# Retention attention and a capacity-limited expert layer on one core: the planned VectorE times behind each routing list, and the last eviction in two halves

## The chip, the cores and the metric

The kernel runs on one core of a Trainium2 chip, as one program. The metric is the device time of one execution in microseconds (us). Before the change three executions took 613.02, 613.28 and 613.60 us (median 613.28). The trace comes from one further execution under the hardware profiler: its own time was 615.13 us, its span (first to last recorded instruction) 613.3 us.

## The reference, cut to what matters

```python
scores = scale * np.matmul(q, k.transpose(0, 1, 3, 2))      # 8 batches, 8 heads, 576 positions, 64 wide
ret = scores * Dmat[None, :, :, :]                          # gamma_h ** (i - j) for i >= j, else 0
attn = np.matmul(ret, v)                                    # -> x, 4608 tokens x 512
logits = x @ w_gate                                         # 4608 x 8
for idx in np.argsort(-logits.flatten()):                   # best (token, expert) pair first
    tok, e = idx // E, idx % E
    if assigned[tok] >= 0 or counts[e] >= 576:              # a token once, an expert 576 times
        continue
    assigned[tok] = e; counts[e] += 1
for e in range(8):
    out[mask_e] = np.maximum(x[mask_e] @ w1[e], 0) @ w2[e]  # 512 -> 1024 -> 512
```

The order in which pairs are accepted is sequential in the reference. The kernel finds the same assignment by closing one expert at a time: eight searches, each followed by the list of the 576 tokens of the expert that it closed.

## The kernel before, in words

**Stages.** TensorE (PE) computes the attention in the first 130 us or so. Then it runs the experts e = 0 to 7, each as `l1(e)` and `l2(e)`. `l1` makes 16 groups of 12 matmuls (each float32 operand is split in a high and a low part, so that a product is three matmuls), 128x256 and 128x320 in turn, with relu on ScalarE (ACT, L1093) and the low part of the result on VectorE (DVE, `low`, L1056). `l2` makes five tiles `py` of 128x512 (the last of 64 rows); ACT copies each to `yt` (L1155; L1157 and DVE L1158 for the 64 rows), and GpSimd (POOL) scatters the rows to the output by an indirect DMA (L1113). The last expert takes its tiles in the order 4, 0, 1, 2, 3.

**Routing.** `phases()` is one long generator that alternates between DVE work and small bf16 matmuls on PE. For p = 0 to 6 a search runs: rounds `it` in which DVE builds a matrix of comparisons `G` (L174), PE sums it with 9 matmuls (L350, result `r`), and DVE decides (L354 to L366). Then the list of the expert found: DVE builds `rh` and `G`, PE runs L458 and L461 into `r`, DVE turns `r` into the row numbers `idx` (L468 to L472) and, for list 5 onwards, `quart` (L477, L479), by which POOL gathers the tokens. Then `leave(p)` (L504 to L515) takes the expert and its tokens out of play, and `best` (L208 to L220) finds each token's best expert that is left, which opens the next search.

**What sets the order.** Each `yield ns, pe` of the generator names a planned DVE time since the last yield, and a planned PE time of the matmuls behind it. A planner (`Mixer`) keeps two planned clocks, one for PE and one for DVE. After each few matmuls of `l1` and `l2` it advances the PE clock (`mix.adv`), and when the planned DVE clock says that the operands are ready it puts the generator's next small matmuls into PE's queue, and the DVE work behind them into DVE's queue. So the planned times alone decide after how many expert matmuls a routing matmul stands on PE, and what stands ahead of what on DVE. All queues run in the order written; nothing is reordered on the chip.

**The tokens of an expert.** Experts 0 to 4 have their tokens transposed on PE (`pt`, L1038; low part by DVE L1041). Experts 5 to 7 (`QUART` = 5) have them gathered in 18 quarter gathers and transposed on DVE in five pieces (four of 128x4x128, the last 128x4x64): DVE L1020 makes `xt`, ACT L1022 copies it to `xh`, and DVE L1013 subtracts to make `xl`, one piece behind. The pieces are put into the queues one by one during `l2` of the expert before when their planned arrival is past, and what is left is put there at the start of `l1` without a further condition. The first group of `l1` (256 tokens) needs pieces 0 and 1, the second (320 tokens) the others too.

Of the kernel before, what the change touches and what calls it, by code (L numbers as in the profile page):

```python
# [16 lines left out]
AF = mybir.ActivationFunctionType  # L17
# [4 lines left out]
N, DM, E, FF = 4608, 512, 8, 1024  # L22
SLACK = 1.0
QUART = 5
# [46 lines left out]
def widths(shifts):  # L71
    return [1 << (a - b) for a, b in zip([32] + shifts[:-1], shifts)]
# [16 lines left out]
class Route:  # L89
# [232 lines left out]
    def search(s, p):  # L322
        nc, V, pool, ps = s.nc, s.nc.vector, s.pool, s.ps
        SH, KK = LATER, widths(LATER)
        for _ in s.ordered():
            pass
        s.dig(0)
        for it, K in enumerate(KK):
            last = it == len(SH) - 1
            v2 = pool.tile([128, 36, 2], BF16, name="v", bufs=2)  # L330
            v = v2[:, :, 0]
            if it:

                V.tensor_scalar(v2, u[:, :, None].to_broadcast([128, 36, 2]), j, float(K), op0=ALU.subtract, op1=ALU.mult)
            else:
                V.tensor_copy(v2, s.dg[:, 0, :, None].to_broadcast([128, 36, 2]))
            s.reach(0, 36, K, v2, ALU.is_le)
            if it == 0:
                for k in range(1, 7):
                    s.dig(k)  # L340
                for a, b in ((1, 4), (4, 7)):
                    V.tensor_scalar(s.D[:, a:b], s.dg[:, a:b], 1.0/KK[a], None, op0=ALU.mult)
            if not last:
                u = pool.tile([128, 36], F32, name="u")
                V.tensor_tensor(u, v, s.D[:, it+1], op=ALU.add)

            yield (2050 + 19*K if it else 1350 if p > 1 else 350), 310
            cp = ps.tile([128, 32], F32, name="r")
            for c in range(0, 36, 4):
                nc.tensor.matmul(cp, s.G[:, c:c+4].rearrange("p c k -> p (c k)"), s.oh[:, c:c+4, :], start=(c == 0), stop=(c == 32))  # L350
            own = [cp[32*c:32*c+32, 8*c:8*c+8] for c in range(4)]

            cs = pool.tile([32, 8], F32, name="cs")
            V.scalar_tensor_tensor(cs, s.nr[:32], -1.0, own[0], op0=ALU.mult, op1=ALU.subtract)  # L354
            for x in own[1:3]:
                V.tensor_tensor(cs, cs, x, op=ALU.subtract)
            for q in range(0, 128, 32):
                V.tensor_tensor(s.f[q:q+32, :8], own[3], cs, op=ALU.is_ge)
            if last:
                break  # L360

            mq = pool.tile([128, 1], F32, name="mq")
            tc, j = pool.tile([128, 32], F32, name="tc"), pool.tile([128, 1], F32, name="j")
            V.tensor_reduce(mq, s.f[:, :8], axis=AX.X, op=ALU.max)
            V.transpose(tc, mq.to_broadcast([128, 32]))
            V.tensor_reduce(j, tc[:, 1:K], axis=AX.X, op=ALU.add)  # L366

        tf, cf = pool.tile([128, 32], F32, name="tc"), pool.tile([128, 32], F32, name="cf")
        nk, nf = pool.tile([128, 1], F32, name="nk"), pool.tile([128, 1], F32, name="nf")
        w = pool.tile([128, 8], F32, name="w8")  # L370
        s.ge = pool.tile([128, 2, 36], F32, name="ge")
        s.gt, s.eq = s.ge[:, 0], s.ge[:, 1]
        V.transpose(tf, s.f)
        V.tensor_reduce(nk, tf[:, :K], axis=AX.X, op=ALU.add)
        V.transpose(cf, nk.to_broadcast([128, 32]))
        V.tensor_reduce(nf, cf[:, :8], axis=AX.X, op=ALU.max)
        V.scalar_tensor_tensor(w, cf[:, :8], nf, s.dec, op0=ALU.is_equal, op1=ALU.mult)
        V.tensor_scalar(s.gt, v, nf, -1.0, op0=ALU.subtract, op1=ALU.is_gt)
        V.tensor_scalar(s.eq, v, nf, -1.0, op0=ALU.subtract, op1=ALU.is_equal)
        s.pick(w)  # L380
# [116 lines left out]
    def leave(s, p):  # L497

        nc, V, pool, ps = s.nc, s.nc.vector, s.pool, s.ps
        if p == 0:  # L500
            s.taken()
        e = pool.tile([128, 8], F32, name="eb")
        a = pool.tile([128, 36], F32, name="gone")
        V.tensor_scalar(e, s.es, -2*BIG, BIG, op0=ALU.mult, op1=ALU.add)  # L504
        V.scalar_tensor_tensor(a, s.q, CAP - HALF, s.mem[:, 1], op0=ALU.is_lt, op1=ALU.mult)
        V.tensor_tensor(s.Lg, s.Lg, e[:, None, :].to_broadcast([128, 36, 8]), op=ALU.min)
        V.tensor_tensor(a, a, s.gt, op=ALU.add)
        if p == 0:
            V.tensor_scalar(s.cap, a, -2*BIG, BIG, op0=ALU.mult, op1=ALU.add)
            V.tensor_tensor(s.acc, s.gt, s.mx8, op=ALU.mult)  # L510
        else:
            V.tensor_scalar(a, a, -2*BIG, BIG, op0=ALU.mult, op1=ALU.add)
            V.tensor_tensor(s.gt, s.gt, s.mx8, op=ALU.mult)
            V.tensor_tensor(s.cap, s.cap, a, op=ALU.min)
            V.tensor_tensor(s.acc, s.acc, s.gt, op=ALU.add)  # L515
        if p == 0:
            yield 1550, 100
            cn = ps.tile([128, 8], F32, name="r")
            nc.tensor.matmul(cn, s.ones, s.n8, start=True, stop=True)
        for _ in s.best(capped=True):  # L520
            pass
        if p == 0:
            s.room(cn)
        yield (2400 if p == 0 else 5000 if p == 1 else 3500 if p < QUART else 4700), 0

def attention(tc, nc, P, qk, vk, cst_d, er_d, wg_d, rf, xd, Lg):
    cst = P['a'].tile([128, CST], F32, name="cst")
# [376 lines left out]
def moe(tc, nc, P, R, xd, w1_d, w1q_d, w2_d, out, mix):  # L904
    V, A, T = nc.vector, nc.scalar, nc.tensor
# [66 lines left out]
    def conv(by=None):  # L972

        conv_hi()
        conv_lo(by)
# [143 lines left out]
    def l2(e, hb):  # L1119
        tr = iter(())  # L1120
        late = []
        want = 4*(e + 1 < E)
        wait = 0
        for t in range(5) if e < E - 1 else (4, 0, 1, 2, 3):
            n = 128 if t < 4 else 64
            ps = P['ps'].tile([128, DM], F32, name="py", tag="y", bufs=2)
            c = slice(128*t, 128*t+n)
            k, last = 0, 23 if t < 4 else 15
            for f in range(8):
                wh, wl = [w[:, (f % 2)*512:(f % 2)*512+512] for w in W2[e, f // 2]]  # L1130

                h = hb[:, f]
                for a, w in ((h[:, c], wh), (h[:, 640+128*t:768+128*t], wh), (h[:, c], wl)) if t < 4 else \
                        ((h[:, 512:640], wh), (h[:, c], wl)):
                    m = a.shape[1]
                    T.matmul(ps[:m], a, w, start=(k == 0), stop=(k == last), skip_group_check=True)  # L1136
                    k += 1
                mix.adv(650 if t < 4 else 430)
                if owed and f == 1:
                    owed.pop()()  # L1140
                gather(e + 1)
                wait -= 1

                soon = state['listing'] == e + 1 and not ready(e + 1)
                if want and wait <= 0 and e + 1 in regs and not soon:
                    conv()
                    want, wait = want - 1, 6
                if late and not soon:
                    late.pop(0)()
                if e + 1 in XG and e + 1 not in XH and mix.t > state['arrives']:  # L1150
                    tr = transposes(e + 1)
                next(tr, None)
            y = P['w'].tile([128, DM], F32, name="yt", bufs=3)
            if t < 4:
                A.activation(y, ps, AF.Copy)  # L1155
            else:
                A.activation(y[:n], ps[n:], AF.Copy)  # L1157
                V.tensor_tensor(y[:n], y[:n], ps[:n], op=ALU.add)  # L1158
            late.append(lambda t=t, y=y, n=n: scatter(e, t, y, n))
        if QUART - 1 <= e + 1 < E - 1:  # L1160
            behindhand.extend(late)
        else:
            for f in late:
                f()
        for _ in range(want):
            conv()
        if e + 1 < E:
            mix.drain(lambda: ready(e + 1))
            gather(e + 1, True)
            if e + 1 not in XH:  # L1170
                tr = transposes(e + 1)
        return tr
# [105 lines left out]
```

## Time and profile before

| | |
|---|---|
| three executions, median | 613.28 us |
| profiled execution, its own time | 615.13 us |
| its span | 613.3 us |
| PE busy | 597.1 us (97% of the span) |
| DVE busy | 421.0 us (69%) |
| ACT busy | 289.4 us (47%) |
| POOL busy | 187.9 us (31%) |

Experts' `l1` start on PE at about 222.6 (e = 1), 280, 338, 395.9, 451.74 (e = 5), 503.8 and 555 us. The lists' matmuls (L458) start at 202.6, 251.2, 298.5, 346.7, 395.25, 441.8 and 459 us for lists 1 to 7. In a matmul row of the timeline the duration includes the time to run through the array, so matmuls that follow each other start closer together than their rows are long (128x512 rows of 0.39 us follow each other by 0.23). Idle time in front of a row is counted from the modelled end of the one before. The execution's own time is 1.83 us longer than its span (615.13 − 613.3).

### The profile page before, as it was taken

The numbers are of one execution on the slowest core, as the hardware profiler recorded it, in microseconds if no ns is written. First come the engines' busy times: TensorE is split into PE (matmuls) and PEld (weight loads), VectorE is DVE, ScalarE is ACT, GpSimd is POOL, SyncE is SP. The second block draws the span as 40 slices with busy tenths as digits, with TensorE's granted clock in tenths as the row PEclk, the third lists the DMA queues.
The fourth block names the chain that finished last, engine by engine and source line by source line (L and its number), as shares of the span: only waits on it lengthen the run. The fifth ranks groups of instructions, "written<-read, shape, count | busy, mean of one in ns | idle before, by whom it ended". The sixth has DMA issues, their size and how long they took to land.

```text
span 613.3 us, 14831 instructions
## 1 busy us (share of the span) xinstructions
PE 597.1 (97%) x5711; PEld 509.9 (83%) x5715; DVE 421.0 (69%) x1545; ACT 289.4 (47%) x585; POOL 187.9 (31%) x260
## 2 busy tenths in 40 slices
PE   8999999998999999999999999999999999999995
PEld 5888887775698889879977998799889889989984
DVE  3688989898799878978886897799884323312300
ACT  4555555551364456433552447154536636634410
POOL 0000000000511442341432233257727746862121
PEclk9999999999999999999999999999999999999998
DMA  9999999924477699694988298649858995994611
GB/s 322 401 374 324 390 364 383 328 82 161 138 187 146 214 251 227 201 241 137 218 226 233 63 246 209 204 83 253 207 170 170 234 260 121 248 251 139 125 39 39
DMA packets 51504, 132.05 MB, mean 215 GB/s; under 512 B 6352, under 2 KB 20304, under 8 KB 51432
## 3 DMA queue, kind: packets, MB, share of 16 engines
q0 software_dynamic: 15296, 50.87, 37.5%
q1 hardware_dynamic: 35812, 79.77, 37.4%
q8 instruction: 45, 0.74, 0.5%
q10 hardware_dynamic: 324, 0.45, 0.2%
q14 instruction: 27, 0.22, 0.1%
HBM read 80.21 MB, written 18.87 MB: 162 GB/s over the span
## 4 chain that ended last, share of the span: by engine, by line
PE 74%; DVE 12%; issue 7%; DMA 3%; POOL 2%; ACT 1%; POOLq 0%; SPq 0%; ACTq 0%; DVEq 0%
PE ph L1083 24%; PE py L1136 24%; PE pA L598 6%; PE pX L642 5%; PE pS L621 3%; PE pX L633 2%; DVE hb L1056 2%; PE pT L680 2%; POOL xg L989 2%; PE r L350 1%; DMA out_y<-yt,idx 1%; DVE G L174 1%; PE pT L694 1%; PE pt L1038 1%; PE pXt L650 1%
## 5 line engine op out<-in xcount | busy, mean ns | idle before, releaser
L1136 PE MATMUL py<-w2h,hb 128*128 128x512 f32 x576 | 186.8, 396 | 0.0
L1083 PE MATMUL ph<-xh,w1h 128*128 128x320 f32 (+1 forms) x512 | 151.4, 301 | 0.7 <-issue 0.4
L1083 PE MATMUL ph<-xl,w1h 128*128 128x320 f32 (+1 forms) x512 | 148.6, 296 | 0.0
L1083 PE MATMUL ph<-xh,w1l 128*128 128x320 f32 (+1 forms) x512 | 148.5, 296 | 0.0
L1136 PE MATMUL py<-w2l,hb 128*128 128x512 f32 (+1 forms) x320 | 125.1, 391 | 0.0
L1136 PEld LDWEIGHTS py<-w2h,hb 128*128 128x128 f32 x576 | 104.9, 188 | 22.4
L1093 ACT ACTIVATE hb<-ph 128x256 fp32r<-128x256 f32 (+1 forms) x128 | 52.2, 408 | 104.8 <-PE ph L1083 94.5
L1083 PEld LDWEIGHTS ph<-xh,w1h 128*128 128x128 f32 x512 | 95.9, 189 | 2.4 <-issue 1.5
L1083 PEld LDWEIGHTS ph<-xl,w1h 128*128 128x128 f32 x512 | 96.1, 190 | 0.6 <-DVE xl L1041 0.3
L1083 PEld LDWEIGHTS ph<-xh,w1l 128*128 128x128 f32 x512 | 96.0, 190 | 0.0
L1056 DVE SCALAR_TENSOR_TENSOR hb<-ph,hb 128x256 fp32r<-128x256 f32 (+1 forms) x192 | 58.2, 352 | 45.7 <-ACT hb L1093 38.0
L989 POOL DMA_INDIRECT xg<-xd,idx x25 | 25.8, 1031 | 188.4 <-ACT w1h L957 153.8
L1113 POOL DMA_INDIRECT out_y<-yt,idx x40 | 40.5, 1012 | 89.7 <-ACT yt L1155 59.2
L1136 PEld LDWEIGHTS py<-w2l,hb 128*128 128x128 f32 (+1 forms) x320 | 56.7, 177 | 12.7
L1155 ACT ACTIVATE yt<-py 128x512 f32<-128x512 f32 x32 | 19.1, 596 | 86.6 <-PE py L1136 55.8
L1000 POOL DMA_INDIRECT xg<-xd,quart x54 | 54.6, 1011 | 15.3 <-issue 12.3
L967 POOL DMA_DIRECT2D w2l<-raw x32 | 30.1, 954 | 73.2 <-ACT hb L1093 72.5
L582 ACT ACTIVATE vin<-vin,cst 128x128 f32<-128x128 f32 (+1 forms) x160 | 48.2, 380 | 6.5 <-DMA vin<-in_vk 4.3
L600 DVE TENSOR_TENSOR am<-pA,cst 128x1024 f32<-128x1024 f32 x32 | 38.8, 1213 | 11.4 <-PE pA L598 11.1
L967 POOL DMA_DIRECT2D w1l<-raw x29 | 27.5, 963 | 43.5 <-ACT w1l L966 30.6
L598 PEld LDWEIGHTS pA<-qin,kin 64*128 64x128 f32 x512 | 31.6, 189 | 9.4 <-issue 3.5
L623 ACT ACTIVATE S<-pS 128x128 f32<-128x128 f32 x64 | 17.8, 278 | 42.9 <-PE pS L621 42.6
(193 smaller groups left out, 907.5 us busy)
## 6 DMA issues: line engine op xcount, KB each, us to landing
raw<-in_w SPq DMA_DIRECT2D x52, 512.0 KB, 5.4
w2l<-raw POOLq DMA_DIRECT2D x32, 512.0 KB
w1l<-raw POOLq DMA_DIRECT2D x29, 512.0 KB
kin<-in_qk SPq DMA_DIRECT2D x14, 576.0 KB
qin<-in_qk SPq DMA_DIRECT2D x14, 576.0 KB, 7.5
vin<-in_vk SPq DMA_DIRECT2D x14, 576.0 KB
nin<-in_vk SPq DMA_DIRECT2D x14, 512.0 KB, 8.7
xd<-xr SPq DMA_DIRECT2D x36, 192.0 KB, 7.8
```

The lines of the kernel that those rows point to most:

```text
L582: nc.scalar.activation(x, x, AF.Copy, scale=vs[:, u % HP, 4*c+h:4*c+h+1])
L598: nc.tensor.matmul(pa[:, r, j], LD[u, 'k'][half(r), s], LD[u, 'q'][half(r), s], start=True, stop=True, skip_group_check=True)
L600: nc.vector.tensor_tensor(AM[u, hf], pa, m1[:, None, None, :].to_broadcast([128, 2, 4, 128]), op=ALU.mult)
L642: nc.tensor.matmul(PX[u, hf][half(h), b, 128*c:128*c+128], v[:, a:a+64], AM[u, hf][:, h ^ b, j], start=False, stop=False, skip_group_check ...
L967: nc.gpsimd.dma_start(lo, raw, accum_op=ALU.add)
L989: nc.gpsimd.indirect_dma_start(out=xg[:n, 4*j:4*j+4, :].rearrange("p a c -> p (a c)"), out_offset=None, in_=xd[:, :], in_offset=bass.Indir ...
L1000: nc.gpsimd.indirect_dma_start(out=XG[e][:, g, :], out_offset=None, in_=xq, in_offset=bass.IndirectOffsetOnAxis(ap=lines[e][:, g:g+1], axi ...
L1056: V.scalar_tensor_tensor(hb[:, f, to+a:to+b], ps[:, a:b], 0.0, hb[:, f, 256*s+a:256*s+b].bitcast(F32), op0=ALU.max, op1=ALU.subtract)
L1083: T.matmul(ps, w, x, start=(k == 0), stop=(k == 11))
L1093: A.activation(hb[:, f, c], ps, AF.Relu)
L1113: st = nc.gpsimd.indirect_dma_start(out=out[:, :], out_offset=bass.IndirectOffsetOnAxis(ap=found[e][:n, t:t+1], axis=0), in_=y[:n], in_off ...
L1136: T.matmul(ps[:m], a, w, start=(k == 0), stop=(k == last), skip_group_check=True)
```

## The change

Four planned times change, none in the first lists: the first matmul of a search from p = 2 on is planned for 1500 instead of 1350 ns, the second round of a search from p = 3 on for 350 ns more. `leave` from p = 2 on gets a yield of 1100 ns ahead of its operations and another ahead of `best`, and its last yield becomes 1300 instead of 3500 (p = 2 to 4) or 2000 instead of 4700 (p = 5, 6). A yield with a PE time of 0 has no matmul behind it; it lets the planner put expert work between the pieces. And the last tile of the last expert is copied out in two halves, columns 0 to 255 by ACT, 256 to 511 by DVE.

```diff
-            yield (2050 + 19*K if it else 1350 if p > 1 else 350), 310
+            yield (2050 + 19*K + 350*(it == 1 and p > 2) if it else 1500 if p > 1 else 350), 310
@@ leave
         if p == 0:
             s.taken()
+        if p > 1:
+            yield 1100, 0
         e = pool.tile([128, 8], F32, name="eb")
@@ leave
             nc.tensor.matmul(cn, s.ones, s.n8, start=True, stop=True)
+        elif p > 1:
+            yield 1100, 0
         for _ in s.best(capped=True):
             pass
         if p == 0:
             s.room(cn)
-        yield (2400 if p == 0 else 5000 if p == 1 else 3500 if p < QUART else 4700), 0
+        yield (2400 if p == 0 else 5000 if p == 1 else 1300 if p < QUART else 2000), 0
@@ l2
-            if t < 4:
+            if t == 3 and e == E - 1:
+                A.activation(y[:, :DM//2], ps[:, :DM//2], AF.Copy)
+                V.tensor_copy(y[:, DM//2:], ps[:, DM//2:])
+            elif t < 4:
                 A.activation(y, ps, AF.Copy)
```

Line numbers up to 501 stay, then they grow by 2, by 4 from 520 on, and by 7 behind the changed lines of `l2`.

The rows below are instructions in the order in which they stand in an engine's queue. In DVE's queue, the list of expert 6 before the change (`r` is the matmuls' result, `lo`, `tk`, `idx` and `quart` make the row numbers, `eb` opens `leave`, `oh` ends `best`, `xt` and `xl` are expert 5's transposed tokens):

```order
L479 TENSOR_SCALAR quart<-tk 32x4x5 x4
L504 TENSOR_SCALAR eb<-es 128x8
...
L220 TENSOR_TENSOR oh<-t_536,mx_537 128x288
L1020 STREAM_TRANSPOSE xt<-xg 128x4x128
L1013 TENSOR_TENSOR xl<-xt,xh 128x4x128
L1020 STREAM_TRANSPOSE xt<-xg 128x4x64
L1013 TENSOR_TENSOR xl<-xt,xh 128x4x128
L1013 TENSOR_TENSOR xl<-xt,xh 128x4x64
L398 TENSOR_SCALAR w_7154<-room 128x8
```

And the same place after the change:

```order
L1024 STREAM_TRANSPOSE xt<-xg 128x4x128
L1017 TENSOR_TENSOR xl<-xt,xh 128x4x128
L494 TENSOR_TENSOR room<-room,r 128x8
...
L479 TENSOR_SCALAR quart<-tk 32x4x5 x4
L1024 STREAM_TRANSPOSE xt<-xg 128x4x64
L1017 TENSOR_TENSOR xl<-xt,xh 128x4x128
L1165 TENSOR_TENSOR yt<-yt,py 64x512
L1017 TENSOR_TENSOR xl<-xt,xh 128x4x64
L506 TENSOR_SCALAR eb<-es 128x8
```

The last piece of expert 5 stood behind list 6, `leave` and `best`, and stands directly behind the list now, with `leave` behind it. In PE's queue, the end of the same list's matmuls before the change (`n` is the count of tokens taken, `py` a tile of `l2(4)`):

```order
L458 MATMUL r<-rh,G 128x160
L461 LDWEIGHTS ones
L461 MATMUL r<-n_7019,ones 128x8
L1136 MATMUL py<-w2h,hb 128x512 x2
L1136 MATMUL py<-w2l,hb 128x512
```

And after the change (`ph` is the first group of `l1(5)`, 12 matmuls of 128x256, of which the first and the last are shown, and then the first two of the second group):

```order
L1140 MATMUL py<-w2l,hb 64x512
L458 LDWEIGHTS G
...
L461 MATMUL r<-n_7069,ones 128x8
L1087 MATMUL ph<-xh,w1h 128x256
...
L1087 MATMUL ph<-xh,w1l 128x256
L1087 MATMUL ph<-xh,w1h 128x320
L1087 MATMUL ph<-xl,w1h 128x320
```

The list's matmuls have moved from the middle of `l2(4)` to its end: what stands behind them is no longer `l2` but the first group of the next expert. At the end of the program, DVE and ACT after the change, with what each waits for (the numbers behind names are those of semaphores):

```order
L1165 TENSOR_TENSOR yt<-yt,py 64x512 [waits DMASW0_49,Activation_49]
L1160 COPY yt<-py 128x256 [waits DMASW1_49,DMASW2_49,DMASW0_49,Activation_49]
```

```order
L1162 ACTIVATE yt<-py 128x512 [waits DMASW7_49,DVE_49,PE_49]
L1159 ACTIVATE yt<-py 128x256 [waits DMASW0_49,PE_49,Activation_49]
```

The DVE half waits for an ACT instruction, and the ACT half for PE: the two halves stand one behind the other, where one ACT instruction of 128x512 (L1155) stood before.

## Rows read from the trace of the kernel before

**Rows 1.** Windows by stage; columns window, length, busy us of each engine, clock, DMA
```profile
250.00:350.00 100.00, 98.62 (x693) 84.21 (x693) 82.16 (x358) 44.25 (x69) 32.60 (x44) 1.00 0.71 186
350.00:450.00 100.00, 99.28 (x693) 86.37 (x692) 86.39 (x375) 47.10 (x73) 47.56 (x66) 1.00 0.81 205
450.00:600.00 150.00, 150.00 (x907) 135.65 (x906) 46.28 (x132) 70.81 (x115) 74.33 (x108) 1.00 0.68 170
```

**Rows 2.** Waits of PE between 250 and 450 us; total us, times, longest
```profile
PE r L350 <- DVE G L174: 1.2, 3, 0.7
PE r L350 <- issue: 0.3, 1, 0.3
PE ph L1083 <- DVE hb L1056: 0.2, 1, 0.2
PE ph L1083 <- issue: 0.2, 1, 0.2
PE pt L1038 <- DVE v L334: 0.2, 1, 0.2
```

**Rows 3.** Timeline of PE behind list 2; start, length, instruction, [idle before]
```profile
251.87 0.17 PE L461 MATMUL r<-n,ones 128*128 128x8 bf16 x1
...
258.58 0.39 PE L1136 MATMUL py<-w2l,hb 128*128 128x512 f32 x1
259.68 0.39 PE L350 MATMUL r<-oh,G 128*128 128x32 bf16 x9 [0.72 <-DVE G L174]
```

**Rows 4.** Timeline of PE, list 6 and the start of expert 5
```profile
442.49 0.71 PE L1136 MATMUL py<-w2h,hb 128*128 128x512 f32 x2
...
451.74 0.28 PE L1083 MATMUL ph<-xh,w1h 128*128 128x256 f32 x1
...
453.16 0.31 PE L1083 MATMUL ph<-xh,w1h 128*128 128x320 f32 x1
453.31 0.31 PE L1083 MATMUL ph<-xl,w1h 128*128 128x320 f32 x1
```

**Rows 5.** Timeline of DVE from list 6 on
```profile
442.69 0.16 DVE L494 TENSOR_TENSOR room<-room,r 128x8 f32<-128x8 f32 x1 [0.36 <-PE r L461]
...
444.97 0.74 DVE L479 TENSOR_SCALAR quart<-tk 32x20 int32<-32x20 f32 x4
...
450.34 0.43 DVE L1020 STREAM_TRANSPOSE xt<-xg 128x256 f32<-128x256 f32 x1
450.70 0.99 DVE L1013 TENSOR_TENSOR xl<-xt,xh 128x512 fp32r<-128x512 f32 x2
...
453.66 0.68 DVE L1158 TENSOR_TENSOR yt<-yt,py 64x512 f32<-64x512 f32 x1
```

**Rows 6.** Timeline of ACT at the start of expert 5
```profile
450.81 0.42 ACT L1022 ACTIVATE xh<-xt 128x256 fp32r<-128x256 f32 x1 [0.30 <-DVE xt L1020]
...
451.99 0.59 ACT L1157 ACTIVATE yt<-py 64x512 f32<-64x512 f32 x1 [0.27 <-ACT yt L1155]
453.42 0.38 ACT L1093 ACTIVATE hb<-ph 128x256 fp32r<-128x256 f32 x1 [0.84 <-PE ph L1083]
```

**Rows 7.** Timeline of all engines at the end, and a DVE read of 128x256 earlier
```profile
465.02 0.42 DVE L1056 SCALAR_TENSOR_TENSOR hb<-ph,hb 128x256 fp32r<-128x256 f32 x1 [0.99 <-ACT hb L1093]
...
606.04 0.60 ACT L1155 ACTIVATE yt<-py 128x512 f32<-128x512 f32 x1 [4.89 <-PE py L1136]
606.92 0.97 POOL L1113 DMA_INDIRECT out_y<-yt,idx  x1 [4.43 <-ACT yt L1155]
```

**Rows 8.** Windows behind PE's last matmul, columns as in the first group
```profile
606.00:610.00 4.00, 0.00 (x0) 0.00 (x0) 0.00 (x0) 0.60 (x1) 0.97 (x1) 0.98 0.17 66
610.00:613.30 3.30, 0.00 (x0) 0.00 (x0) 0.00 (x0) 0.00 (x0) 0.00 (x0) 0.50 0.00 0
```

**Rows 9.** Timeline of PE at the start of the program
```profile
1.48 3.17 PE L1224 MATMUL warm<-full 128*128 128x512 bf16 x7 [1.48 <-DVE full L1211]
...
6.32 0.82 PE L1224 MATMUL warm<-full 128*128 128x512 bf16 x3
```

## The prediction, made before the changed kernel ran

> **What bounds the kernel now.** I read the table of busy shares first: PE 97%, DVE 69%, ACT 47%, so the end is set by PE's queue, and the question is only where PE stands still. The windows by stage answer it [rows 1]: from 450 us on PE is busy for all of 150.00 us, between 250 and 450 it lacks 1.38 + 0.72 = 2.10 us. Nothing behind 450 us can absorb a delay, and nothing there can be gained either: what PE wins or loses before 450 us, or at any place after it, goes to the end one for one. The third view, PE's waits in these 200 us, has seven waits with 2.1 us in sum [rows 2]; four of them are at L350, the first matmuls of a search, which come just behind a list. The timeline of the longest [rows 3] shows that a wait is worth more than its bracket: matmuls of `l2` follow each other at 0.23 us (30 of them lie between 251.9 and 258.8), but their rows are 0.39 long, so from 258.58 the next could start at 258.81 and starts at 259.68, 0.87 later where the bracket says 0.72. With 0.15 more for each of seven, the waits cost 2.1 + 1.05 = 3.15 us. That is all that a better order of the routing can win.
>
> **The cause of the waits.** Behind list 2 PE has 30 expert matmuls in its queue, 6.9 us, and DVE needs from 251.87 to 259.68, 7.8 us, for the list's rows, `leave`, `best` and the first `G` [rows 3]. The planner believed less, so it put the search's matmul too early.
>
> **Part 1, the planned times.** They add no instruction; they move the small matmuls, and DVE's work with them, along the expert work. Counted in the changed queue, behind list 2 now stand 39 expert matmuls instead of 30: 39 × 0.23 = 9.0 us against the 7.8 needed, so that wait is gone. Behind list 3 the cover grows from 8.2 to 9.5 us, behind list 4 from 8.9 to 9.2, behind list 5 from 9.7 to 10.4 (numbers of matmuls times 0.12, 0.15 or 0.23 by their width). The DVE chain there also has `low` operations of 0.42 [rows 7] between its parts, and with lists 4 and 5 the new cover is only 0.3 and 0.7 longer. I leave 0.1 to 0.2 of wait at each of these two, and about 0.35 (0.2 by its bracket and 0.15) at a transposition on PE that waits behind the search on DVE [rows 2], which the new times don't touch: 0.65 in all. Gain 3.15 − 0.65 = **2.5 us**; the bounds are 3.15 (all waits gone) and 0 (each comes back elsewhere).
>
> **What the moves trigger.** The planned totals are longer now for each list, so everything behind list 2 drifts along the expert work. List 6's matmuls stood in the middle of `l2(4)`, 9.3 us ahead of expert 5 (442.49 to 451.74) [rows 4], and DVE had done the list, `leave`, `best` and the last two pieces of expert 5's tokens while PE worked on `l2(4)`. Now the list's matmuls are the last thing before `l1(5)`, and on DVE the last piece (128x4x64) stands behind the list's rows. The second group of `l1(5)` needs that piece. So PE must wait for DVE to do the whole list, and the price can be worked out from durations of before. Let S be the start of the matmul that stands directly behind L461: 442.49 in the trace, the first of `l1(5)` in the changed queue.
> DVE's first operation on the list starts 0.20 behind S (442.69), the last (`quart`) ends at 444.97 + 0.74 = 445.71, S + 3.22 [rows 5]. The piece's transposition takes 0.43: S + 3.65. ACT's copy to `xh` starts 0.04 later (450.34 + 0.43 to 450.81) and takes 0.42: S + 4.11 [rows 5, 6]. PE's 13th matmul, the first of the second group, is due at S + 1.42 (453.16 − 451.74) [rows 4]: it waits **2.7 us**.
> The 14th needs `xl` of that piece. DVE has the earlier piece's subtraction first (0.99 for the two of 512 and 256, less 0.42 for the second: 0.57, to S + 4.22), then the addition of the 64-row tile, whose ACT copy of 0.59 stands behind `xh` (to S + 4.70), 0.68 long (to S + 5.4), then its own 0.42: S + 5.8 [rows 5, 6]. PE is there at S + 4.11 + 0.15 = 4.26 [rows 4]: it waits **1.5 us**.
> Together **4.2 us**. The lower bound is 2.7, if the second wait has other work ahead of it done sooner; the upper 4.6, if DVE comes to the list 0.4 late because an earlier piece is in front of it. I take 4.2, the sum of the rows. Nothing hides it, since PE has no other work in its queue there. What is queued behind the waiting matmul is all of `l1(5)`; ACT and DVE wait for its results, and they have room after 450 us (DVE busy for 46 of 150 us, ACT for 71 [rows 1]).
>
> **What else is shifted.** `leave` is now behind the last piece on DVE instead of ahead of it; search 6, list 7 and the gathers of experts 6 and 7 on POOL's queue come some 10 us later. Expert 6 starts 52 us after expert 5, so this cover (busy DVE share below a third there) costs nothing; if it were used up, a wait at `l1(6)` would follow. SP's queue holds weight loads, which go by the expert work and don't move against it. I cost these at 0.
>
> **Part 2, the last tile.** Before: the copy of 128x512 takes 0.60, and POOL's scatter follows [rows 7]. After: the DVE half waits for the ACT half, as its wait in the queue shows, and the scatter waits for the DVE half. ACT's 128x256 takes 0.38 [rows 6], a hand-over 0.04 [rows 5, 6], DVE's 128x256 out of PSUM 0.42 [rows 7]: 0.84 for 0.60, **+0.24 us** at the very end, where nothing covers it. If the halves ran side by side it would be 0.42 for 0.60, −0.18; with a hand-over like that of PE to DVE (0.20), +0.40.
> The Trainium skill (PSUM — Partial Sum Buffer, "PSUM bank collisions raise a hardware error") speaks against this part: two engines may not read the same bank of the same 32 partitions at once, even in different columns, and the compiler's scheduler therefore puts a dependency between ACT and DVE. By that rule side by side is excluded and the halves are worth a loss; the wait in the queue agrees, and no run here shows a read side by side.
>
> **The sum.** −2.5 + 4.2 + 0.24 = +1.9 us. Made against the profiled execution's own time: 615.13 + 1.9 = 617.0. That execution is 1.85 above the median of the runs (613.28), which carry no profiler; carried over, the forecast is 613.28 + 1.9 = **615.2 us**. What a measurement of this kernel can tell from no change is about 0.2%, 1.2 us.
>
> **Rivals.**
> A, the forecast, 615.2, chance 0.57. Its own range is 614.2 to 616.0: gain 2.0 to 3.15, stall 3.8 to 4.6.
> B, faster: the stall at expert 5 is hidden. That needs DVE to have the last piece done before the list, or the list's chain to run in 1.4 us instead of 3.2. The order of both queues speaks against it, since the piece stands behind `quart` and `quart` behind PE's L461. The time would be 613.28 − 2.5 + 0.24 = 611.0. It decides if PE's 13th matmul waits less than 1 us. Chance 0.07.
> C, only the first half of the stall: the addition of the 64-row tile or the earlier subtraction is done in time and the 14th matmul finds `xl`. 613.28 − 2.5 + 0.24 + 2.7 = 613.7. For it: ACT's order may let the 64-row copy run early. Against it: the DVE order has the addition ahead of the subtraction. Chance 0.13.
> D, the clock: PE stands still for 2.7 and, one matmul later, for 1.5 us, longer than the longest wait between 250 and 450 us (0.7 [rows 2]). Behind PE's last matmul the granted clock is 0.98 in the first four us and 0.50, the lower level of 1.2 GHz, only then [rows 8]. If it fell in the stall, a stretch like the one at the start would follow: seven matmuls of 128x512 at 0.45 each (3.17 / 7), and three at 0.27 (0.82 / 3) from 6.32 on [rows 9]; the lower level there lasts 3.2 to 4.8 us, which loses half of it, about 2.0. 615.2 + 2.0 = 617.2. Chance 0.12.
> The Trainium skill (TensorE: Matmul & The Clock Gate, Part 1) has the rule: the clock is a gate that falls back to its lower state when the engine idles and opens after renewed activity. The rows at the end agree that it falls in idleness; none shows a fall inside this kernel's expert stage.
> E, the change doesn't do what it says: half of the waits return at other places, because the drift brings other `low` operations in front of the search. 615.2 + 1.25 = 616.4. For it: lists 4 and 5 gain so little cover. Chance 0.11.
>
> **How the numbers follow.** A range for 8 in 10 takes in A, most of C and E and part of D: 613.5 to 617.0. Faster by over 1.2 us (below 612.05): B alone, 0.07. Within 1.2 us: C (613.7) and the low edge of A, 0.13 + 0.08 = 0.21. Slower (above 614.5): the rest of A, D and E, 0.49 + 0.12 + 0.11 = 0.72.
>
> **What the profile after would show.** Right: no wait at L350 behind lists 2 and 3; in PE's row at the start of `l1(5)` a wait of about 2.5 us in front of the first 128x320 matmul, ended by ACT's `xh`, and another of about 1.3 one matmul later, ended by DVE's `xl`; DVE's `quart` ending some 1.8 us after PE's last 128x256 there; at the end ACT's 0.38, DVE's 0.42 and the scatter in a row. PE's windows from 500 us on full again, at a clock of 1.00. Wrong: a full PE at 440 to 460 us (B); one wait instead of two (C); a PEclk below 1.00 near 450 us (D); new waits between 300 and 440 us of more than 1 us in sum (E).

## The result, and the profile after

The changed kernel took 619.31 us (median of 6 runs, 618.16 to 621.55), the kernel before 613.43 (613.02 to 613.88): a ratio of 1.0096, 95% interval 1.0083 to 1.0108. It is 5.9 us slower, where 1.9 were forecast and 617.0 was the upper end of the range. The direction was right; the time is above even that of rival D (the clock, 617.2).

The profiled execution of the changed kernel has a time of its own of 619.03 us and a span of 617.3. Starts of PE's matmuls in the two timelines divide the spans, which the page rounds to 0.1 us (times in us):

| stretch of PE | before | after | difference |
|---|---|---|---|
| span's start to the first matmul of expert 0 | 162.00 | 160.60 | −1.40 |
| to the first of expert 5 | 289.74 | 287.62 | −2.12 |
| `l1(5)` | 26.45 | 33.35 | +6.90 |
| `l2(5)` to the last matmul's start | 127.38 | 127.38 | 0.00 |
| from there to the end of the span | 7.73 | 8.35 | +0.62 |

The first line is not the change's doing: no order changes there. Without it the profile has +5.4 us, and nearly all of it is in `l1(5)`.

The windows by stage after, as in [rows 1] (window, length, busy us of PE, PEld, DVE, ACT and POOL, clock, DMA):

```profile
250.00:350.00 100.00, 100.00 (x709) 86.97 (x708) 79.82 (x346) 47.09 (x73) 34.13 (x44) 1.00 0.74 191
350.00:450.00 100.00, 99.81 (x695) 85.58 (x693) 84.09 (x365) 45.04 (x70) 48.50 (x63) 1.00 0.81 206
450.00:600.00 150.00, 146.30 (x871) 132.77 (x872) 50.86 (x154) 69.64 (x113) 73.98 (x106) 0.98 0.66 164
```

PE's idle time between 250 and 350 us is gone (1.38 before), and behind 450 us, where there was none, it has 3.70 and a mean clock of 0.98. The waits of PE from 200 us on, the answer to [rows 2]:

```profile
PE ph L1087 <- ACT xh L1026: 2.7, 1, 2.7
PE ph L1087 <- DVE xl L1017: 1.1, 1, 1.1
PE r L350 <- DVE G L174: 0.7, 1, 0.7
```

The timeline of PE at the start of expert 5 [rows 4]:

```profile
448.22 0.36 PE L1087 MATMUL ph<-xh,w1h 128*128 128x256 f32 x1
...
449.61 0.28 PE L1087 MATMUL ph<-xh,w1l 128*128 128x256 f32 x1
452.57 0.54 PE L1087 MATMUL ph<-xh,w1h 128*128 128x320 f32 x1 [2.67 <-ACT xh L1026]
454.24 0.63 PE L1087 MATMUL ph<-xl,w1h 128*128 128x320 f32 x1 [1.13 <-DVE xl L1017]
454.67 0.47 PE L1087 MATMUL ph<-xh,w1l 128*128 128x320 f32 x1
454.93 0.47 PE L1087 MATMUL ph<-xh,w1h 128*128 128x320 f32 x1
...
459.25 0.41 PE L1087 MATMUL ph<-xh,w1h 128*128 128x256 f32 x1
459.47 0.32 PE L1087 MATMUL ph<-xl,w1h 128*128 128x256 f32 x1
```

Start to start the 13th matmul comes 2.84 us late (452.57 − 449.61 − 0.12) and the 14th 1.52 (454.24 − 452.57 − 0.15): 4.36 of the 6.90. Of the rest 0.09 is in the first group (448.22 to 449.61 + 0.12, 1.51 where it was 1.42), and 2.45 is in the matmuls behind the 14th: a 128x320 follows the one ahead of it after 0.26 (454.67 to 454.93) where it took 0.15 before [rows 4], until about 459.5. The windows of two us show why:

```profile
450.00:452.00 2.00, 0.00 (x0) 0.00 (x0) 1.84 (x11) 0.00 (x0) 0.00 (x0) 1.00 0.43 156
452.00:454.00 2.00, 0.54 (x1) 0.19 (x1) 1.47 (x4) 1.40 (x3) 0.21 (x1) 0.67 0.00 0
454.00:456.00 2.00, 1.76 (x6) 1.77 (x7) 1.72 (x10) 0.00 (x0) 1.19 (x1) 0.50 0.00 0
456.00:458.00 2.00, 2.00 (x10) 2.00 (x10) 0.00 (x0) 0.43 (x1) 0.00 (x0) 0.50 0.12 33
458.00:460.00 2.00, 2.00 (x12) 2.00 (x12) 1.89 (x7) 0.07 (x2) 1.17 (x2) 0.62 0.00 0
```

PE is empty from 450 to 452 us, the granted clock falls from 1.00 to 0.50 (the level of 1.2 GHz) between 452 and 454, and comes back between 458 and 460; in windows of half a us it is at 0.50 from about 452.7 to 459.5. The Trainium skill (TensorE: Matmul & The Clock Gate, Part 1) has the clock as a gate that falls back when the engine idles and opens again behind activity; the trace agrees, with 0.50 granted behind the stall and about 1.00 again from 459.5 on.

VectorE's timeline shows the order that makes the stall [rows 5]:

```profile
450.84 0.75 DVE L479 TENSOR_SCALAR quart<-tk 32x20 int32<-32x20 f32 x4
451.62 0.45 DVE L1024 STREAM_TRANSPOSE xt<-xg 128x256 f32<-128x256 f32 x1
451.99 0.65 DVE L1017 TENSOR_TENSOR xl<-xt,xh 128x512 fp32r<-128x512 f32 x1
453.17 0.68 DVE L1165 TENSOR_TENSOR yt<-yt,py 64x512 f32<-64x512 f32 x1 [0.53 <-ACT yt L1164]
453.77 0.41 DVE L1017 TENSOR_TENSOR xl<-xt,xh 128x256 fp32r<-128x256 f32 x1
```

The end of the list (it began at 448.57 with L494), then the last piece, then the addition of the 64-row tile, then the last subtraction, without a gap but for the one on ACT. The third wait of the list above, in the timeline of PE and of DVE in search 2:

```profile
223.75 0.28 PE L1087 MATMUL ph<-xh,w1l 128*128 128x256 f32 x1
224.74 0.39 PE L350 MATMUL r<-oh,G 128*128 128x32 bf16 x9 [0.71 <-DVE G L174]
```

```profile
221.32 0.42 DVE L1045 TENSOR_TENSOR xl<-pt,xh 128x256 fp32r<-128x256 f32 x1 [4.28 <-ACT xh L1044]
221.66 0.14 DVE L354 SCALAR_TENSOR_TENSOR cs<-room,r 32x8 f32<-32x8 f32 x1
...
223.92 0.76 DVE L174 TENSOR_TENSOR G<-ct,v 128x1152 bf16<-128x1152 bf16 x1
```

DVE stands still for 4.28 us in front of expert 1's last low part, with search 2's next round (L354 to L174) behind it. The kernel before has the round ahead of that low part, and no wait; that the move from 1350 to 1500 put it there is tested in experiment 7. The wait costs 0.71 by its bracket and 0.87 start to start (224.74 − 223.75 − 0.12).

### The profile page after: what moved, and what is told of

Same layout as the page of the kernel before. It is cut to its first block, busy times and chain, and to the rows that moved or that the text cites. A ratio compares the mean times of both kernels' runs of the same rounds, so it can differ in the third digit from the quotient of the medians.

```text
span 617.3 us, 14824 instructions
## 1 busy us (share of the span) xinstructions
PE 599.1 (97%) x5711; PEld 511.9 (83%) x5715; DVE 421.3 (68%) x1546; ACT 288.7 (47%) x585; POOL 190.4 (31%) x257
## 4 chain that ended last, share of the span: by engine, by line
PE 81%; DVE 7%; issue 6%; DMA 3%; ACT 1%; POOL 1%; POOLq 0%; DVEq 0%; SPq 0%; ACTq 0%
PE ph L1087 29%; PE py L1140 27%; PE pA L602 5%; PE pX L646 4%; PE pS L625 3%; PE pX L637 2%; DMA qin<-in_qk 2%; PE r L350 2%; PE pt L1042 1%; PE pT L684 1%; PE r L458 1%; PE warm L1231 1%; PE pT L698 1%; PE pXt L654 1%; POOL out_y L1117 1%
## 5 line engine op out<-in xcount | busy, mean ns | idle before, releaser
L1117 POOL DMA_INDIRECT out_y<-yt,idx x40 | 42.6, 1065 | 76.7 <-ACT yt L1162 37.8
L602 PE MATMUL pA<-qin,kin 64*128 64x128 f32 x512 | 37.5, 286 | 0.7 <-DMA qin<-in_qk 0.6
```

What stands on the lines that cost most here:

```text
L602: nc.tensor.matmul(pa[:, r, j], LD[u, 'k'][half(r), s], LD[u, 'q'][half(r), s], start=True, stop=True, skip_group_check=True)
L1117: st = nc.gpsimd.indirect_dma_start(out=out[:, :], out_offset=bass.IndirectOffsetOnAxis(ap=found[e][:n, t:t+1], axis=0), in_=y[:n], in_off ...
```

## The experiments

Every time is a median and stands against runs of the kernel before on the same chip, 613.33 us in the first four and 613.40 in the last four. The ratio is to that kernel, with its 95% interval.

**1. The last tile copied whole**, all planned times changed:

```diff
-            if t == 3 and e == E - 1:
-                A.activation(y[:, :DM//2], ps[:, :DM//2], AF.Copy)
-                V.tensor_copy(y[:, DM//2:], ps[:, DM//2:])
-            elif t < 4:
+            if t < 4:
```

> The changed kernel without the halved copy: the last tile goes out in one ScalarE copy as before; all planned times are the changed ones. Theory (the loss is the stall at expert 5 with the clock's fall behind it; the halves cost 0.24 us): 619.3 - 0.24 = 619.1 us, and the stretch from PE's last matmul to the end of the span back from 8.35 to about 7.7-8.1 us. Rival (the halves carry the whole 0.6 us by which the stretch behind PE's last matmul grew, or more): 618.7 or less. The stall (2.8 and 1.5 us before the 13th and 14th matmul of expert 5) stays in both.

618.28 us, ratio 1.0085 (1.0069 to 1.0100). Most of the loss is not in the copy: at least 4.2 us stay (0.69% of 613). The median is on the rival's side (618.7 or less), and the interval, 617.6 to 619.5 us, takes in both values. In the trace the stall and the clock's fall are there again (`l1(5)` 33.14 us), and the stretch from PE's last matmul to the end is 8.04 us, 0.31 shorter than in the changed kernel.

**2. The halved copy alone**, in the kernel before:

```diff
-            if t < 4:
+            if t == 3 and e == E - 1:
+                A.activation(y[:, :DM//2], ps[:, :DM//2], AF.Copy)
+                V.tensor_copy(y[:, DM//2:], ps[:, DM//2:])
+            elif t < 4:
```

> The kernel before with the halved copy of the last tile as its only edit. Theory: 613.4 + 0.24 = 613.7 us, ScalarE half 0.38, VectorE half 0.42 behind it, scatter 0.24 us later than before. Rival (0.6 us): 614.0. Rival (side by side, a gain of 0.18): 613.2.

613.90 us, ratio 1.0015 (1.0005 to 1.0024), 0.3 to 1.5 us slower. The end of this kernel and that of the first experiment, timelines of all engines:

```profile
604.58 0.38 ACT L1155 ACTIVATE yt<-py 128x256 f32<-128x256 f32 x1 [4.89 <-PE py L1136]
605.00 0.42 DVE L1156 COPY yt<-py 128x256 f32<-128x256 f32 x1 [20.89 <-ACT yt L1155]
605.70 0.97 POOL L1113 DMA_INDIRECT out_y<-yt,idx  x1 [4.67 <-DVE yt L1156]
```

```profile
608.93 0.60 ACT L1159 ACTIVATE yt<-py 128x512 f32<-128x512 f32 x1 [4.89 <-PE py L1140]
609.80 0.97 POOL L1117 DMA_INDIRECT out_y<-yt,idx  x1 [4.43 <-ACT yt L1159]
```

From ACT's start to the scatter's it is 1.12 us with halves and 0.87 in one piece: 0.25, as worked out. The halves don't overlap (DVE starts 0.04 behind ACT's end). From the scatter's start to the end of the span it takes 6.40 here, 6.70 in the first experiment, 6.75 in the changed kernel and 6.38 before, so the 0.3 to 0.4 more of the changed kernel's trace goes with neither form of the copy. Whether the halves cost 0.25 or 0.6 these runs don't decide; that they are a loss they do.

**3. PE kept busy in the stall**, everything else as in the changed kernel:

```diff
+                if e == 5 and i == 1 and k < 2:
+                    P['fill']((12, 6)[k])     # matmuls of 128x512, constant bf16 data, bank "t"
                 T.matmul(ps, w, x, start=(k == 0), stop=(k == 11))
```

> The changed kernel with 12 and 6 extra matmuls of 128x512 (bf16, constant data, into a PSUM bank that is free there) in PE's queue in front of the 13th and the 14th matmul of expert 5: 2.7 and 1.4 us of work, a little shorter than the two waits (2.84 and 1.52 us). PE waits for the same data as before, but isn't idle meanwhile. Theory (the granted clock falls because PE stands still in this stall, and costs 2.5 us in the 7 us behind it): clock 1.00 all through, 619.3 - 2.5 = 616.8 us. Rival (the clock falls for another reason, or the longer matmuls behind the stall are slow by late data): no change, 619.3.

616.76 us, ratio 1.0052 (1.0038 to 1.0066). PE's timeline, and its window from 448 to 462 us:

```profile
450.14 2.54 PE L1239 MATMUL fill<-full 128*128 128x512 bf16 x11
452.66 0.41 PE L1089 MATMUL ph<-xh,w1h 128*128 128x320 f32 x1
452.92 1.47 PE L1239 MATMUL fill<-full 128*128 128x512 bf16 x6
454.33 0.41 PE L1089 MATMUL ph<-xl,w1h 128*128 128x320 f32 x1
454.58 0.31 PE L1089 MATMUL ph<-xh,w1l 128*128 128x320 f32 x1
454.73 0.31 PE L1089 MATMUL ph<-xh,w1h 128*128 128x320 f32 x1
```

```profile
448.00:462.00 14.00, 13.93 (x95) 11.33 (x94) 11.76 (x51) 5.40 (x10) 2.56 (x4) 1.00 0.21 78
```

(The first row counts 11 of the 12 matmuls.) The data come as late as in the changed kernel: the 14th matmul starts 5.93 us behind the first of `l1(5)`, 6.02 there and 1.57 before. But the clock is 1.00 and the matmuls behind follow at 0.15. `l1(5)` takes 30.91 us instead of 33.35. So the fall comes from PE's standing still, and costs about 2.5 us (2.44 by `l1(5)`, 2.55 by the medians).

**4. The last piece ahead of the list**, one planned number of the changed kernel:

```diff
-            state['at'][g] = mix.t + 13000
+            state['at'][g] = mix.t + 11000
```

> The changed kernel with one planned number changed: the arrival of a gathered quarter is planned 11 instead of 13 us after its issue, so that the last piece of expert 5 stands in VectorE's queue ahead of list 6 and not behind it. Theory (the place of this piece makes the stall, and the stall the clock's fall): both waits and the fall are gone, 619.3 - 4.36 - 2.5 = 612.4 us. Rival (another wait takes its place at expert 5: the low parts of the first group, which stand behind the list now, hold PE up at the third group by about 1.2 us): 613.6. Rival (PE waits there for the list's or the gather's data whatever the order): 619.

612.60 us, ratio 0.9991 (0.9980 to 1.0002). DVE's timeline (the subtractions are now ahead of L494), the one wait of PE that is left from 190 us on (the one in search 2), and PE's window from 448 to 462 us:

```profile
450.15 1.06 DVE L1017 TENSOR_TENSOR xl<-xt,xh 128x512 fp32r<-128x512 f32 x2
451.12 0.15 DVE L494 TENSOR_TENSOR room<-room,r 128x8 f32<-128x8 f32 x1
```

```profile
PE r L350 <- DVE G L174: 0.7, 1, 0.7
```

```profile
448.00:462.00 14.00, 14.00 (x108) 13.50 (x107) 13.23 (x55) 8.22 (x15) 5.89 (x10) 1.00 0.47 138
```

`l1(5)` takes 26.54 us, as before the change. The number holds for the gathers of experts 6 and 7 too, but `l2(5)` to the last matmul takes 127.39 us as before, so what changed is at expert 5: both waits and the fall hang on the place of one piece. No wait came at the third group. The loss is gone; a gain on the kernel before is not shown, since the interval takes in 1.

**5. The leave pieces alone**, with the searches and the copy of before (the edit of the copy is not shown here, nor in 6 and 8):

```diff
-            yield (2050 + 19*K + 350*(it == 1 and p > 2) if it else 1500 if p > 1 else 350), 310
+            yield (2050 + 19*K if it else 1350 if p > 1 else 350), 310
```

> Only the leave edit: leave in three pieces with the short planned times; the searches' planned times and the last copy are those of before. Behind list 6 PE's queue has some 20 matmuls of l2(4), 4.7 us, ahead of expert 5, and the last piece stands directly behind the list on VectorE. Theory (the drift that makes the stall comes from the longer planned searches; leave's pieces shorten the wait behind list 2, where 36 expert matmuls now stand, 8.2 us for 7.8 needed, and little else): no stall at expert 5, clock 1.00, 613.4 - 0.9 = 612.5 us. Rival (the leave pieces make the stall): 617 to 618.

611.77 us, ratio 0.9973 (0.9959 to 0.9987): 0.7 us less than expected. PE's waits:

```profile
PE r L350 <- DVE G L174: 1.0, 3, 0.4
```

Seven waits have become three. There is no stall at expert 5 (`l1(5)` 26.45). The shorter planned total and the pieces between which expert work can stand are worth about 1.6 us; I had this part too low.

**6. The longer planned searches alone**, with `leave` and the copy of before (p is never above 7, so the two new yields never come):

```diff
-        if p > 1:
+        if p > 99:
             yield 1100, 0
...
-        elif p > 1:
+        elif p > 99:
             yield 1100, 0
...
-        yield (2400 if p == 0 else 5000 if p == 1 else 1300 if p < QUART else 2000), 0
+        yield (2400 if p == 0 else 5000 if p == 1 else 3500 if p < QUART else 4700), 0
```

> Only the searches' planned times (1500 instead of 1350, and 350 more for the second round); leave and the last copy are those of before. Behind list 6 PE's queue has 12 matmuls of l2(4), 2.8 us, ahead of expert 5, but leave and best (some 3.4 us on VectorE) stand ahead of the last piece. Theory: a first wait of 2.84 - 2.8 + 3.4 = 3.5 us or somewhat more, the second only about 0.3 (the addition is not in front of the subtraction here), the clock falls with it (2.5 us), the wait of 0.87 in search 2 is there, and most of the waits behind the lists are gone (2.5): 613.4 - 2.5 + 0.9 + 3.8 + 2.5 = 618.1 us. Rival (the stall needs the leave pieces): 612.

618.53 us, ratio 1.0075 (1.0052 to 1.0099). PE's waits, its timeline behind the first of them, and two windows after it:

```profile
PE ph L1087 <- ACT xh L1026: 3.2, 1, 3.2
PE r L350 <- DVE G L174: 1.2, 2, 0.7
```

```profile
453.82 0.41 PE L1087 MATMUL ph<-xh,w1h 128*128 128x320 f32 x1 [3.19 <-ACT xh L1026]
...
455.11 0.31 PE L1087 MATMUL ph<-xh,w1h 128*128 128x320 f32 x1
455.25 0.43 PE L1087 MATMUL ph<-xl,w1h 128*128 128x320 f32 x1
455.48 0.47 PE L1087 MATMUL ph<-xh,w1l 128*128 128x320 f32 x1
```

```profile
456.00:458.00 2.00, 2.00 (x10) 2.00 (x10) 1.69 (x9) 0.44 (x1) 0.85 (x2) 0.50 0.14 33
458.00:460.00 2.00, 2.00 (x15) 2.00 (x14) 0.42 (x1) 0.38 (x1) 0.99 (x1) 0.83 0.12 33
```

The stall and the fall come with the searches' times. The time came out near the 618.1 expected, but not term by term: `l1(5)` takes 31.71 us, 5.26 more than before, of which the two late matmuls make 3.35 and 0.31 start to start, so the fall cost only 1.6 in this trace, not 2.5. The clock was at 0.50 from about 455.3 to 458.7 here, half as long as in the changed kernel, so the price of a fall is not one number. By the medians the leave pieces alone win 1.6, the searches alone lose 5.1, and both together, with the copy whole, lose 4.9 (experiment 1). That this is more than the sum of the two, 3.5, is hardly clear of the three intervals.

**7. Search 2 back at 1350**, else the changed kernel:

```diff
-            yield (2050 + 19*K + 350*(it == 1 and p > 2) if it else 1500 if p > 1 else 350), 310
+            yield (2050 + 19*K + 350*(it == 1 and p > 2) if it else 1500 if p > 2 else 1350 if p > 1 else 350), 310
```

> The changed kernel with one number taken back: search 2 keeps its 1350. Its order is that of before up to there (no wait of 0.87 in search 2), and behind list 6 now stand 6 matmuls of l2(4), 1.4 us, ahead of expert 5; the last subtraction stands ahead of the addition. The stall shrinks from 2.84 + 1.52 to about 1.4 + 0.3 us. If the clock stays up in a stall of this length: 619.3 - 0.9 - 2.6 - 2.5 = 613.3 us. If it falls in any stall at this place: 615.8. I expect the former, since PE stood idle for 1.26 us at 107 us in the trace of before without a fall.

613.36 us, ratio 0.9990 (0.9977 to 1.0004). PE's waits, and the windows around the first:

```profile
PE ph L1087 <- ACT xh L1026: 1.2, 1, 1.2
PE r L350 <- DVE G L174: 0.4, 1, 0.4
```

```profile
445.00:450.00 5.00, 3.99 (x30) 3.13 (x28) 4.64 (x21) 1.44 (x3) 0.99 (x1) 1.00 0.70 241
450.00:455.00 5.00, 4.80 (x33) 4.58 (x34) 4.67 (x18) 1.90 (x5) 2.35 (x4) 1.00 0.06 14
```

The wait that is left at L350 is a new one, at 409 us; the one in search 2 is gone. A stall of 1.3 us and 0.3 behind it (start to start), where the changed kernel has 2.84 and 1.52, leaves the clock at 1.00. This one number, which puts six matmuls between the list and expert 5 and frees search 2, is worth 5.9 us.

**8. Tuned by these runs**: leave in pieces, search 2 as before, arrival after 11 us, one copy of the last tile, and

```diff
-            yield (2050 + 19*K + 350*(it == 1 and p > 2) if it else 1500 if p > 1 else 350), 310
+            yield (2050 + 19*K + 350*(it == 1 and p > 2) if it else 1700 if p > 2 else 1350 if p > 1 else 350), 310
```

> What the runs so far point to: leave in three pieces, search 2 as before, the first matmul of searches 3 to 6 planned for 1700 (1500 in the change), their second round for 350 more, arrival of gathered quarters planned after 11 instead of 13 us, and the last tile copied whole. Theory: the waits behind the lists gone but for about 0.5 us, no wait in search 2, no stall, clock 1.00, no loss at the end: 613.4 - 2.6 = 610.8 us. Rival (the waits removed come back as others, since the low parts and pieces move too): 612.6 as with the piece first, or more.

610.83 us (610.29 to 611.24), ratio 0.9946 (0.9926 to 0.9967), 0.5% faster than the kernel before and clear of its runs. Its windows:

```profile
250.00:350.00 100.00, 100.00 (x713) 86.86 (x712) 79.65 (x346) 46.78 (x73) 34.56 (x44) 1.00 0.72 186
350.00:450.00 100.00, 99.98 (x699) 86.62 (x697) 84.92 (x370) 45.65 (x72) 48.00 (x65) 1.00 0.82 208
```

PE lacks 0.02 us of these 200, and nothing from 450 to 600 us: what the change could win is won here, about 2.6 us.

## Why the prediction was wrong

**What bounds the kernel: right.** `l2(5)` to the last matmul takes 127.38 us in both traces; what PE lost before went to the end in full.

**The waits behind the lists (−2.5): nearly right.** Of 3.15 us of waits some 0.25 are left in the changed kernel's trace (between 400 and 420 us, where search 5 opens). To the start of expert 5 it wins 2.12; with the 0.87 of search 2 that is 3.0 of removed waits, near the upper bound of the term. The wait at the transposition, which I had left standing with 0.35, went too.

**"What else is shifted ... I cost these at 0": wrong by 0.87.** I counted the cover behind each list and didn't look at what stands ahead of a search's round on DVE. In search 2 the round came to stand behind a low part of expert 1 for which DVE waits 4.28 us, and had to wait with it. Experiment 7 takes this away with one number.

**The stall at expert 5 (4.2): right.** 2.84 and 1.52 us where 2.7 and 1.5 were worked out, released by ACT's `xh` and DVE's `xl` as said; experiment 4 removes both by moving the piece.

**The clock: the step that failed.** The sum went by a clock of 1.00 through a stall of 4.2 us, and the fall was a rival at 0.12. Experiment 3 shows it as a term of 2.5 us (2.0 were worked out for it), and every run of the changed kernel has a mean clock of 0.991 to 0.993, those of the kernel before 0.996 to 0.998. I read the windows at the end [rows 8] as showing that PE can stand still for four us at 0.98; in the changed kernel the clock was at 0.50 by about 452.7, with PE idle from 449.89 to 452.57. The trace of before had no stall in the expert stage longer than 0.7 us (and one of 1.3 in the attention, at 107 us, that left the clock at 1.00), so this one place at the end was all that spoke for the clock staying up through the two waits that I had worked out myself. Rival D's fall belonged in the sum.

**The last tile (+0.24): right as a hand-over (0.25), perhaps too low as a whole** (0.57 between medians, interval 0.3 to 1.5). Not all of the 0.62 in the table is the copy's. The stretch from the scatter's start to the end of the span is 6.4 us in the four traces with neither or only one of the two edits of planned times, and 6.7 in the six with both, whatever the copy. Why is open.

**The sum.** By the trace −3.0 + 0.87 + 4.36 + 0.09 + 2.45 + 0.62 = +5.4, by the medians +5.9; the remaining 0.5 is within what single runs differ by (618.16 to 621.55). The forecast lacks 2.45 of the clock, 0.87 of search 2 and 0.4 at the end, and has the gain 0.5 too small. Its step from the profiled execution to the median was right in size for a wrong reason: the profiler costs nothing visible (619.03 against a median of 619.31 after), but the profiled execution of before had a slow start, 162.0 us to expert 0, where the other nine traces have 160.1 to 161.6.

## What to carry to other kernels

A longer planned time is not a local edit: it moves all that follows against the other queues, so look where each moved chain lands, above all what stands behind it on its engine and is needed at once. When a stall of several us on TensorE follows from the working, put the clock's fall into the sum, and remember that idle PE time can be bridged by spare matmuls (2.5 us won back in experiment 3). And split a sum's test into its parts: here a loss of 6.9 us in one place hid a gain of 3.0, and 2 us in one planned number took that loss away (experiment 4).

## What the runs showed of the hardware

The clock's fall need not show inside the stall. In the changed kernel it comes at about 452.7, just behind the end of the first wait (452.57). In experiment 6 PE stood still for 3.2 us, took up its work at 453.82 and was soon at full pace, and slowed only at 455.25, when it had been at work again for 1.4 us. Nor is its price fixed: the clock was at 0.50 for 6.8 us in the changed kernel, which cost 2.45, and for 3.4 in experiment 6, which cost 1.6. In the six runs of that experiment the three with a mean clock of 0.993 or 0.994 took 617.3 to 617.8 us, the three with 0.992 took 619.2 to 619.6. Behind waits of 1.2 us (experiment 7) and 0.7 us (search 2) the clock stayed at 1.00. The scatter at the end takes 6.4 or 6.7 us from its start to the end of the span, whichever engine it waited for.
